# Turning the last two products of a decode block around: weights as the moving operand, four column groups

## The chip, the cores and the metric

One core of one Trainium2 chip. The metric is device time in microseconds (us); lower is better. Times are medians of several executions, and all of them are fast unless a line says otherwise. A ratio of two kernels is the mean time of one kernel's fast runs over the mean of the other's in the same rounds on the same chip, so it is not quite the ratio of the medians that are quoted. All intervals are 95%.

## The reference, cut to what matters

A gated mix of a cached attention block and a mixer MLP, for two rows (batch 2, one position), D = 1024, 32 heads of 128, 16384 cached keys a head, F = 3584, everything in bf16:

```python
g = sigmoid((x * gate_w).sum(-1, keepdims=True))
a = attention(x @ wq, k_cache, v_cache).reshape(B, Sq, H * Dh) @ wo      # wo: 4096 x 1024
x1 = x + shift_mix(gelu(layernorm(x) @ w1)) @ w2
b = x1 + gelu(layernorm(x1) @ w3) @ w4                                  # w4: 3584 x 1024
return g * a + (1 - g) * b
```

The two caches are 537 MB of the 573 MB that are read. The two products at the end, with `w4` and `wo`, give two rows of 1024 outputs. Of a matmul's two operands, the kernel's `lhsT` is called *stationary* here and its `rhs` *moving*; the page lists the load of the stationary one as PEld and the matmul itself as PE, 5589 of each before the change. The sums stand in tiles of the pools in PSUM.

## The kernel before

Everything that is loaded in bulk goes through a ring of three buffers of 64 KB a partition (`big`). A load *lands* when the last of its records of completion comes in the trace; the trace lists each load as *packets*, which the 16 DMA engines move; here a packet is one contiguous piece.

```python
    const = ctx.enter_context(tc.tile_pool(name="const", bufs=1))
    big = ctx.enter_context(tc.tile_pool(name="big", bufs=NBIG))
    tpool = ctx.enter_context(tc.tile_pool(name="tpool", bufs=2))
    # ... cut: other pools
    def load_k(i):
        t = big_tile("Kn")
        nc.sync.dma_start(
            out=t[:].rearrange("p (j d) -> p j d", d=Dh), in_=cache_rows(A_k_cache, i)
        )
    # ... cut
    W4_SPLIT = [7] * 4
    WO_SPLIT = [4] * 6 + [2, 2, 1, 1, 1, 1]     # rows of 256 KB per DMA
```

The tail: `st_down` multiplies by `w4`, the result is added to the residual `x1` and weighted by `1 - g` into `pre`; `wo_stage` multiplies by `wo` and takes `pre` in through the identity. The weights are the stationary operand, and the two batch rows are the moving one: eight matmuls of two columns a weight row.

```python
    def wo_stage():
        # ... cut: Q, the attention rows, transposed and permuted
        wo = wt.pop("wo").rearrange("k r (p c) -> k r p c", c=KC)
        for r in range(32):
            if r == 24:
                nc.tensor.matmul(wo_acc[:]..., lhsT=ident_f[:], rhs=pre[:]..., start=False, stop=False)
            for c in range(KC):
                nc.tensor.matmul(
                    wo_acc[:, c, :], lhsT=wo[:, r, :, c], rhs=Q[:, :, r],
                    start=(r == 0 and c == 0), stop=(r == 31 and c == KC - 1),
                )
    # ...
    xn2T = const.tile([P, KC, B], BF16)
    h2T = const.tile([P, FC, B], BF16)
    pre = const.tile([P, KC, B], FP32)

    def st_down():
        # ... cut: the same eight matmuls a row, with w4 and h2T, into ps
        nc.vector.tensor_tensor(out=pre[:], in0=x1[:], in1=ps[:], op=ALU.add)
        nc.vector.tensor_tensor(out=pre[:], in0=pre[:], in1=over_r(omg_bc[:]), op=ALU.mult)
    # ... at the very end
    out_pm = const.tile([P, B, KC], BF16)
    nc.vector.tensor_copy(out=out_pm[:].rearrange("p b r -> p r b"), in_=wo_acc[:])
    nc.sync.dma_start(out=out.rearrange("b s (p r) -> p (b s) r", p=P), in_=out_pm[:])
```

## Time and profile before

| | before |
|---|---|
| time, median | 1338.44 us |
| span of the profiled run | 1336.7 us |
| read from HBM | 573 MB at 428 GB/s |
| last row of `wo` lands | 1331.84 us |
| last matmul ends | 1333.26 us |
| output DMA issued | 1333.54 us |

The page gives busy time as shares of the span, and then the span in 40 slices; a digit is the busy share of a slice in tenths.

```profile
PE 845.2 (63%) x5589; PEld 403.1 (30%) x5589; DVE 709.2 (53%) x863; ACT 45.6 (3%) x100; POOL 14.2 (1%) x45
...
DMA  9999999999999999999999999999999999999997
...
q1 hardware_dynamic: 12928, 572.54, 99.1%
q8 instruction: 44, 0.72, 0.2%
```

The DMA line is what matters: the 16 DMA engines are busy from end to end, and no compute engine is. The last two lines are queues (packets, MB, share of 16 engines' span): all loads are on one queue of 12928 packets, and the other one, which the page calls `instruction`, carries 44 packets.

The timeline of the tail (start, duration, engine, line, operation, count, and in brackets the idle time before and what ended it):

```profile
1321.91 2.09 PE L406 MATMUL wo_acc<-Q,wo 128*128 128x2 bf16 x32 [0.34 <-DMA wo<-in_A_wo_dram]
1324.36 2.09 PE L406 MATMUL wo_acc<-Q,wo 128*128 128x2 bf16 x32 [0.35 <-DMA wo<-in_A_wo_dram]
1326.80 2.10 PE L406 MATMUL wo_acc<-Q,wo 128*128 128x2 bf16 x32 [0.35 <-DMA wo<-in_A_wo_dram]
1328.76 0.59 PE L398 MATMUL wo_acc<-pre,ident_f 128*128 128x16 f32 x2
1329.19 4.05 PE L406 MATMUL wo_acc<-Q,wo 128*128 128x2 bf16 x64
1333.28 0.23 DVE L557 CAST out_pm<-wo_acc 128x16 bf16<-128x16 f32 x1 [17.16 <-PE wo_acc L406]
1333.54 0.40 SPq L559 DMA_DIRECT2D out_dram<-out_pm  x1
```

And the chain that ended last, from 1303.63 us (start, duration, what):

```profile
1303.63 23.12 DMA wo<-in_A_wo_dram
1326.75 0.05 issue
1326.80 2.10 PE wo_acc L406 x32
1328.90 0.45 PE wo_acc L398 x2
1329.35 3.91 PE wo_acc L406 x64
1333.26 0.02 issue
1333.28 0.23 DVE out_pm L557
```

Up to 1326.75 us the chain is a load. After it PE has no bracket, so it waits for nothing: it has fallen behind the last, small pieces and works them off until 1333.26 us, 1.4 us after the last row has landed. That 1.4 us, the copy and the output are all that is not load time.

### The profile page before, as it was taken

The page shows a single profiled execution, that of the slowest core. Times are in us where ns is not written, and L with a number is a line of the kernel's source. Part 1 is how long each engine was busy: PE and PEld are TensorE (multiplying, and loading weights), DVE is VectorE, ACT ScalarE, POOL GpSimd, SP SyncE. Part 2 cuts the span into 40 slices and gives each one's busy share as a digit, 9 for nine tenths or more (in the row PEclk, how much of TensorE's full clock was granted, in tenths as well). Part 3 has the DMA queues.
Part 4 walks back from the last instruction along what each step waited for, and adds up shares of the span by engine and source line. Part 5 has one row for each costly group of instructions (what it writes and reads, how often), then busy time and mean ns, then how long its engine had stood idle before and what let it go on. Part 6 is the DMA issues. An engine that isn't in the chain of part 4 may idle for free.

```text
span 1336.7 us, 12996 instructions
## 1 busy us (share of the span) xinstructions
PE 845.2 (63%) x5589; PEld 403.1 (30%) x5589; DVE 709.2 (53%) x863; ACT 45.6 (3%) x100; POOL 14.2 (1%) x45
## 2 busy tenths in 40 slices
PE   2577665677657765555766555567656556765568
PEld 2233222433225322222322222233222223322238
DVE  0666565366651665545666545556655455656520
ACT  0000000000000000000000000000000000000000
POOL 0000000000000000000000000000000000000000
PEclk9988777688776877778887777888777788877775
DMA  9999999999999999999999999999999999999997
GB/s 409 436 436 434 422 440 434 429 440 434 422 435 437 440 436 422 430 440 428 438 438 433 430 432 430 440 438 426 434 430 438 438 432 430 434 428 436 434 421 294
DMA packets 12986, 573.37 MB, mean 429 GB/s; under 512 B 2048, under 2 KB 2048, under 8 KB 2816
## 3 DMA queue, kind: packets, MB, share of 16 engines
q1 hardware_dynamic: 12928, 572.54, 99.1%
q8 instruction: 44, 0.72, 0.2%
q14 instruction: 14, 0.11, 0.0%
HBM read 572.53 MB, written 0.00 MB: 428 GB/s over the span
## 4 chain that ended last, share of the span: by engine, by line
PE 29%; DVE 24%; DMA 17%; another core or an unknown queue 14%; issue 13%; ACT 3%; SPq 0%; ACTq 0%; POOL 0%
DVE T L297 20%; PE S L305 15%; DMA Kn<-in_A_k_cache_dram 13%; PE O L349 7%; PE misc L212 2%; PE misc L359 2%; DMA w<-in_B_w_dram 2%; DMA wo<-in_A_wo_dram 2%; PE misc L458 2%; ACT Pr L333 1%; DVE PT L337 1%; ACT Os L357 1%; DVE mx L326 1%; DVE mdiag L319 1%
## 5 line engine op out<-in xcount | busy, mean ns | idle before, releaser
L305 PE MATMUL S<-T,z 128*128 128x512 bf16 x2048 | 596.1, 424 | 325.0 <-DVE T L297 309.9
L297 DVE STREAM_TRANSPOSE T<-Kn 128x1024 f32<-128x1024 f32 x512 | 612.1, 1230 | 264.6 <-DMA Kn<-in_A_k_cache_dram 215.3
L305 PEld LDWEIGHTS <-z 128*128 128x128 bf16 x2048 | 218.7, 107 | 696.9 <-issue 535.0
L349 PE MATMUL O<-Vn,PT 128*32 128x512 bf16 x2048 | 121.4, 390 | 5.0 <-DMA Vn<-in_A_v_cache_dram 5.0
L376 DVE SCALAR_TENSOR_TENSOR OT<-misc,g_bc,rinv 128x2 bf16<-128x2 f32 x32 | 7.0, 220 | 159.2 <-PE misc L359 159.2
L349 PEld LDWEIGHTS <-PT 128*32 128x32 bf16 x2048 | 73.8, 140 | 51.3 <-issue 22.1
L212 PE MATMUL misc<-rs,ones_f 128*128 128x2 f32 x64 | 17.9, 349 | 79.1 <-DVE rs L369 79.1
L357 ACT COPY Os<-O 128x512 f32<-128x512 f32 x32 | 18.8, 586 | 1067.1 <-PE O L349 1067.1
L359 PE MATMUL misc<-osel,Os 128*128 128x2 f32 x256 | 34.5, 257 | 22.2 <-ACT Os L357 22.2
L359 PEld LDWEIGHTS misc<-osel,Os 128*128 128x128 f32 x256 | 31.8, 195 | 37.1 <-ACT Os L357 37.1
L316 DVE TENSOR_REDUCE m<-S 128x1 f32<-128x512 f32 x32 | 22.1, 692 | 36.9 <-PE S L305 36.9
L212 PEld LDWEIGHTS misc<-rs,ones_f 128*128 128x128 f32 x64 | 16.1, 312 | 84.0 <-issue 81.2
L337 DVE STREAM_TRANSPOSE PT<-Pr 128x512 bf16<-128x512 bf16 x32 | 22.8, 711 | 28.7 <-ACT Pr L333 28.7
L212 PE MATMUL misc<-mdiag,ones_f 128*128 128x128 f32 x64 | 15.6, 326 | 16.9 <-DVE mdiag L319 16.9
L333 ACT ACTIVATE Pr<-S,nb 128x512 bf16<-128x512 f32 x32 | 22.0, 687 | 125.2 <-DVE nb L328 122.2
L458 PEld LDWEIGHTS <-wt 128*128 128x128 bf16 x352 | 22.3, 165 | 9.8 <-DMA wt<-in_B_w_dram 8.5
L326 DVE TENSOR_REDUCE mx<-misc 64x1 f32<-64x64 f32 x64 | 14.2, 222 | 18.9 <-PE misc L212 18.5
L250 PE MATMUL misc<-xT,wt 128*128 128x2 bf16 x256 | 7.1, 165 | 25.8 <-DVE xT L245 23.2
L275 POOL TENSOR_TENSOR z<-qsel,own 128x32 bf16<-128x32 bf16 x32 | 10.6, 330 | 1205.4 <-PE S L305 1174.2
L458 PE MATMUL misc<-xn2T,wt 128*128 128x2 bf16 x224 | 14.4, 202 | 8.3 <-DMA wt<-in_B_w_dram 8.3
L373 DVE RECIPROCAL rinv<-misc 128x2 f32<-128x2 f32 x32 | 5.5, 171 | 22.6 <-PE misc L212 22.6
L406 PE MATMUL wo_acc<-Q,wo 128*128 128x2 bf16 x256 | 16.3, 199 | 1.1 <-DMA wo<-in_A_wo_dram 1.1
(76 smaller groups left out, 119.5 us busy)
## 6 DMA issues: line engine op xcount, KB each, us to landing
Vn<-in_A_v_cache_dram SPq DMA_DIRECT2D x2, 4096.0 KB, 47.3
wt<-in_B_w_dram SPq DMA_DIRECT2D x1, 7168.0 KB, 50.3
w<-in_B_w_dram SPq DMA_DIRECT2D x4, 1792.0 KB, 29.1
wo<-in_A_wo_dram SPq DMA_DIRECT2D x6, 1024.0 KB, 30.2
wt<-in_B_w_dram SPq DMA_DIRECT2D x2, 2048.0 KB, 39.6
wo<-in_A_wo_dram SPq DMA_DIRECT2D x2, 512.0 KB, 18.6
wo<-in_A_wo_dram SPq DMA_DIRECT2D x4, 256.0 KB, 12.7
Kn<-in_A_k_cache_dram SPq DMA_DIRECT2D x32, 51.9
```

The lines of the kernel that those rows point to most:

```text
L212: nc.tensor.matmul(ps[:], lhsT=ones_f[:], rhs=src, start=True, stop=True)
L297: nc.vector.transpose(out=T[:].rearrange("p w j s -> p j w s"), in_=Kw[:, m * CW : (m + 1) * CW].rearrange("p (j w e) -> p j w e", w=2, e=32),
L305: nc.tensor.matmul(S[:], lhsT=z[:, v, NM - 1 - m : NM - 1 - m + P], rhs=Tb[:, v // 2, :, v % 2], start=(m == 0 and v == 0), stop=(m == NM ...
L316: nc.vector.reduce_max(out=m[:], in_=S[:], axis=AX.X)
L326: nc.vector.reduce_max(out=mx[pa, :], in_=mall[pa, pa], axis=AX.X)
L333: nc.scalar.activation(out=Pr[:], in_=S[:], func=ACTF.Exp, bias=nb[:], scale=scale, accum_out=rs[:])
L337: nc.vector.transpose(out=PT[:], in_=Pr[:])
L349: nc.tensor.matmul(O[32 * g : 32 * g + 32, :], lhsT=PT[:, m : CJ * 32 : 16], rhs=V[:, j0 : j0 + 4, :], start=(m == 0), stop=(m == NM - 1),)
L357: nc.scalar.copy(out=Os[:].rearrange("p x d -> p (x d)"), in_=O[:])
L359: nc.tensor.matmul(oc[:], lhsT=Os[:, x, :], rhs=osel[:, x, :], start=(x == 0), stop=(x == 3))
L406: nc.tensor.matmul(wo_acc[:, c, :], lhsT=wo[:, r, :, c], rhs=Q[:, :, r], start=(r == 0 and c == 0), stop=(r == 31 and c == KC - 1),)
L458: nc.tensor.matmul(ps[:, c, :], lhsT=w[:, r, :].rearrange("k (p c) -> k p c", c=C)[:, :, c], rhs=actT[:, r, :], start=(r == 0), stop=(r == ...
```

## The change

Its intent: let the weights move instead. A weight row then needs four matmuls of 256 moving columns with a stationary operand of only two columns, and the four write from partitions 0, 32, 64 and 96 on; they are called four column groups here. Both products, and the residual, add up in one PSUM tile. The residual goes in early, through small fp32 matmuls right after `x1` is known, and `1 - g` is multiplied into the gelu. The output leaves as eight rows of 512 bytes, on two queues.

```diff
     OT = const.tile([P, B, H], BF16)
-    wo_acc = acc.tile([P, KC, B], FP32, name="wo_acc")
+    NQ = 4
+    QW = D // NQ
+    out_acc = acc.tile([P, QW], FP32, name="out_acc")
@@
+    def add_row_product(actT, w_row, last=False):
+        for g in range(NQ):
+            nc.tensor.matmul(
+                out_acc[group(g), :],            # partitions 32g and 32g + 1
+                lhsT=actT,
+                rhs=w_row[:, g * QW : (g + 1) * QW],
+                start=False, stop=last, skip_group_check=True,
+            )
+
+    def start_out(x1):
+        # ... cut: four matmuls that clear out_acc
+        res = const.tile([P, KC, B], FP32, name="cen")
+        nc.vector.tensor_tensor(out=res[:], in0=x1, in1=over_r(omg_bc[:]), op=ALU.mult)
+        # ... cut: 32 fp32 matmuls, res against the identity, into out_acc
@@
-        # ... cut: the loop over r and c of wo_stage
+        for r in range(32):
+            add_row_product(Q[:, :, r], wo[:, r, :], last=(r == 31))
@@
-    pre = const.tile([P, KC, B], FP32)
@@ st_down
+        for r in range(FC):
+            add_row_product(h2T[:, r, :], w4[:, r, :])
@@
-    out_pm = const.tile([P, B, KC], BF16)
-    # ... cut: copy and one output DMA
+    rows = t_tile([P, QW], BF16, "rows")
+    nc.vector.tensor_copy(out=rows[:], in_=out_acc[:])
+    for b, queue in enumerate((nc.sync, nc.scalar)):
+        queue.dma_start(
+            out=out[b].rearrange("s (g n) -> (s g) n", g=NQ), in_=rows[b : 96 + b + 1 : 32, :]
+        )
```

More of the change, by code (lines that the diff above doesn't have):

```diff
@@ L383, in pv_stage, with group @@
         )
+    def group(g):
+        return slice(32 * g, 32 * g + B)
+    def add_row_product(actT, w_row, last=False):
[4 more added lines that the diff above has]
+                rhs=w_row[:, g * QW : (g + 1) * QW],
+                start=False,
+                stop=last,
+                skip_group_check=True,
+            )
+    def start_out(x1):
+        for g in range(NQ):
+            nc.tensor.matmul(
+                out_acc[32 * g : 32 * g + 32, :],
+                lhsT=perm[:, 0:32],
+                rhs=shT[:, 0, 0:1].to_broadcast([P, QW]),
+                start=True,
+                stop=False,
+                skip_group_check=True,
+            )
+        res = const.tile([P, KC, B], FP32, name="cen")
+        nc.vector.tensor_tensor(out=res[:], in0=x1, in1=over_r(omg_bc[:]), op=ALU.mult)
+        for c in range(KC):
+            for g in range(NQ):
+                nc.tensor.matmul(
+                    out_acc[group(g), c:QW:KC],
+                    lhsT=res[:, c, :],
+                    rhs=ident_f[:, 32 * g : 32 * g + 32],
+                    start=False,
+                    stop=False,
+                    skip_group_check=True,
+                )
     def wo_stage():
@@ L394, in wo_stage @@
         nc.vector.tensor_copy(out=Q[:], in_=q_ps[:])
-        wo = wt.pop("wo").rearrange("k r (p c) -> k r p c", c=KC)
+        wo = wt.pop("wo")
         for r in range(32):
-            if r == 24:
-                nc.tensor.matmul(
-                    wo_acc[:].rearrange("p c b -> p (c b)"),
-                    lhsT=ident_f[:],
-                    rhs=pre[:].rearrange("p c b -> p (c b)"),
-                    start=False,
-                    stop=False,
-                )
-            for c in range(KC):
-                nc.tensor.matmul(
-                    wo_acc[:, c, :],
-                    lhsT=wo[:, r, :, c],
-                    rhs=Q[:, :, r],
-                    start=(r == 0 and c == 0),
-                    stop=(r == 31 and c == KC - 1),
-                )
+            add_row_product(Q[:, :, r], wo[:, r, :], last=(r == 31))
     def layernorm(src, dst):
@@ L436, in layernorm, with gelu @@
         nc.vector.tensor_tensor(out=dst, in0=cen[:], in1=over_r(rstd[:]), op=ALU.mult)
-    def gelu(pre_f32, dst_bf, C):
+    def gelu(pre_f32, dst_bf, C, weight=None):
         sq = t_tile([P, C, B], FP32, "gelu")
@@ L448, in gelu @@
         )
+        if weight is not None:
+            nc.vector.tensor_tensor(
+                out=sq[:], in0=sq[:], in1=weight.unsqueeze(1).to_broadcast([P, C, B]), op=ALU.mult
+            )
         nc.vector.tensor_tensor(out=dst_bf, in0=sq[:], in1=pre_f32, op=ALU.mult)
@@ L486, in st_mix @@
         layernorm(x1[:], xn2T[:])
+        start_out(x1[:])
     def st_up():
@@ L490, in st_up @@
         nc.vector.tensor_copy(out=h2[:], in_=linear("w3", xn2T)[:])
-        gelu(h2[:], h2T[:], FC)
+        gelu(h2[:], h2T[:], FC, omg_bc[:])
     def st_down():
-        w4 = wt.pop("w4").rearrange("k r (p c) -> k r p c", c=KC)
-        ps = misc_psum([P, KC, B])
+        w4 = wt.pop("w4")
         for r in range(FC):
-            for c in range(KC):
-                nc.tensor.matmul(
-                    ps[:, c, :],
-                    lhsT=w4[:, r, :, c],
-                    rhs=h2T[:, r, :],
-                    start=(r == 0 and c == 0),
-                    stop=(r == FC - 1 and c == KC - 1),
-                )
-        nc.vector.tensor_tensor(out=pre[:], in0=x1[:], in1=ps[:], op=ALU.add)
-        nc.vector.tensor_tensor(out=pre[:], in0=pre[:], in1=over_r(omg_bc[:]), op=ALU.mult)
+            add_row_product(h2T[:, r, :], w4[:, r, :])
     extra = {
@@ L554 @@
     assert not xfers
-    out_pm = const.tile([P, B, KC], BF16)
-    nc.vector.tensor_copy(out=out_pm[:].rearrange("p b r -> p r b"), in_=wo_acc[:])
-    with nc.allow_non_contiguous_dma(reason="4 KB"):
-        nc.sync.dma_start(out=out.rearrange("b s (p r) -> p (b s) r", p=P), in_=out_pm[:])
+    rows = t_tile([P, QW], BF16, "rows")
[3 more added lines that the diff above has]
+            out=out[b].rearrange("s (g n) -> (s g) n", g=NQ), in_=rows[b : 96 + b + 1 : 32, :]
+        )
 _INS = ['A_x', 'A_k_cache', 'A_v_cache', 'A_wq', 'A_wo', 'B_x', 'B_w1', 'B_w2', 'B_w3', 'B_w4', 'gate_w']
```

## The prediction

> **What bounds the kernel now.** Loads. The page shows the 16 DMA engines at 9 tenths or more in 39 of 40 slices, 573 MB at 429 GB/s; PE is busy 63%, DVE 53%. The DMA issues show that a K load is issued 51.9 us and a V load 37.4 us before it lands, while 8.4 MB take about 19 us: work is always queued ahead. Only the stretch after the last landing belongs to compute.
>
> **The tail, from the timeline and the DMA issues in narrow windows.** The wo pieces land at about 1324.3, 1326.75, 1328.0, 1329.2, 1329.85, 1330.6, 1331.2 and, the last row, 1331.9. PE works without a wait from 1326.80 to 1333.25: rows 24 to 31 are 64 matmuls in 4.05 us (0.51 us a row of eight), with the two-pass residual matmul, 0.45 us, ahead of them. PE ends 1.35 us behind the last landing. Then DVE copies 128x16 (0.23 us), and the output DMA, issued at 1333.54, lands 2.4 us later. Granted clock is 0.5 there.
>
> **What the change does.**
> - w4 and wo: 480 matmuls of 2 moving columns become 240 of 256, four to a row in four column groups. The O matmuls run this pattern: at a cold clock 32 of 512 columns took 3.64 us, 0.455 us per four. [...] Estimate for 256 columns: 0.23 to 0.27 us a row, against 0.51 before and a row landing every 0.6 us. PE catches up with the loads; after the last landing four matmuls are left, about 0.4 us. It ends near 1332.3 instead of 1333.25. Gain 0.9 us.
> - Residual: two DVE operations on `pre` (0.17 us each) and the late 0.45 us matmul go. About 70 small PE instructions come near 260 us, an estimated 4 to 6 us. DVE there waits 6.85 us for the next K load, so they fit: no cost. The extra multiply in the second gelu, about 0.2 us: no cost.
> - The last copy is 128x256: 0.43 us, an estimate from the 128x512 PSUM reduction (692 ns). Cost 0.2 us.
> - Output: 256 elements of 16 bytes in one DMA become eight of 512 bytes on two queues: 2.4 us becomes perhaps 2.0 to 2.2. Gain 0.2 to 0.4 us.
> - Instruction loads: the DMA records show 16 KB instruction packets (about 0.9 us of one engine each), one every 8 us in the tail. With half the PE instructions there, two of four vanish; the last landing may come 0 to 0.6 us earlier. Gain 0.2 us, uncertain.
>
> Nearly all of the 15 us or so of PE time saved was hidden under loads.
>
> **Prediction.** 1337.2 us, 8 in 10 between 1336.1 and 1338.4. Faster by over 2%: 0.01; within 2%: 0.98; slower by over 2%: 0.01.
>
> **What would show it.** Right: PE waits for a wo DMA before nearly every late piece; rows at 0.22 to 0.3 us; last PE instruction within 0.6 us of the last landing; loads unchanged; the chain of waits ends with a wo DMA, then PE under 1 us. Wrong: rows near 0.9 us would mean column groups one after the other; a gap in the DMA slices near 260 to 300 us would mean that the new start of the sum delayed a buffer.
>
> **What could make it wrong.** A last landing moved by over 1 us through instruction loads or engine imbalance; serial column groups (estimate: about 20 us later); a larger fixed cost of an output DMA on the ScalarE queue.

The gains and costs come to 1.1 to 1.3 us (0.9 - 0.2 + 0.2 to 0.4 + 0.2), and 1338.4 less 1.2 is the 1337.2 us of the forecast. The "cold clock" of the O matmuls was a granted clock of 0.50 (`before`, 1295.1 to 1299.0 us). Of the estimates, the 4 to 6 us of the residual fit 63 ns for each of 70 matmuls (the tail's 64 took 4.05 us), and the 20 us of serial groups fit 60 rows at 0.9 us where one lands every 0.6 us (18 us). That the output DMA would take 2.0 to 2.2 us, and that two of four late instruction packets would vanish, were guesses.

## The result, and the profile after

1341.29 us (median of 4; 1341.07 to 1341.67) against 1338.45 us (1338.41 to 1338.84): ratio 1.0021, interval 1.0003 to 1.0038. Within 2%, as forecast, but 2.8 us slower instead of 1.2 us faster, and outside the stated range.

The page, same lines (the second queue of output is new):

```profile
PE 830.6 (62%) x5415; PEld 380.9 (28%) x5415; DVE 709.3 (53%) x863; ACT 45.6 (3%) x100; POOL 14.5 (1%) x45
...
DMA  9999999999999999999999999999999999999997
...
q1 hardware_dynamic: 12664, 572.54, 99.1%
q8 instruction: 42, 0.69, 0.2%
...
q10 hardware_dynamic: 8, 0.00, 0.0%
```

The tail's timeline, with the middle left out:

```profile
1328.03 1.02 PE L392 MATMUL out_acc<-wo,Q 128*2 128x256 bf16 x16 [1.42 <-DMA wo<-in_A_wo_dram]
...
1330.49 1.02 PE L392 MATMUL out_acc<-wo,Q 128*2 128x256 bf16 x16 [1.44 <-DMA wo<-in_A_wo_dram]
...
1334.96 0.38 PE L392 MATMUL out_acc<-wo,Q 128*2 128x256 bf16 x4 [0.27 <-DMA wo<-in_A_wo_dram]
...
1335.60 0.39 PE L392 MATMUL out_acc<-wo,Q 128*2 128x256 bf16 x4 [0.25 <-DMA wo<-in_A_wo_dram]
...
1336.04 0.42 DVE L575 CAST rows<-out_acc 128x256 bf16<-128x256 f32 x1 [31.21 <-PE out_acc L392]
1336.49 0.65 SPq L577 DMA_DIRECT2D out_dram<-rows  x1
1336.49 1.35 ACTq L577 DMA_DIRECT2D out_dram<-rows  x1
```

The end of the chain:

```profile
1325.56 10.00 DMA wo<-in_A_wo_dram
1335.56 0.04 issue
1335.60 0.41 PE out_acc L392 x4
1336.01 0.02 issue
1336.04 0.42 DVE rows L575
```

Compute did what was intended. Sixteen matmuls (four rows) now take 1.02 us instead of 2.09 us for the 32 matmuls of before, PE waits for every late piece, and it ends 0.45 us after the last landing instead of 1.4. But the last landing itself moved from 1331.84 to 1335.56 us. The reason is not in the tail, as the SyncE queue's timeline shows. It lists when loads are issued; a load is issued when its buffer is freed, which follows the landings before it (in `before`, SyncE waits 584.6 us at the V loads for DVE's work on a K tile, and 333.2 us for K to land). Before:

```profile
32.93 0.33 SPq L106 DMA_DIRECT2D Vn<-in_A_v_cache_dram  x1
...
95.42 0.33 SPq L95 DMA_DIRECT2D Kn<-in_A_k_cache_dram  x1
...
697.14 0.33 SPq L95 DMA_DIRECT2D Kn<-in_A_k_cache_dram  x1
...
1204.12 0.33 SPq L95 DMA_DIRECT2D Kn<-in_A_k_cache_dram  x1
...
1276.02 1.75 SPq L130 DMA_DIRECT2D w<-in_B_w_dram  x4
```

After:

```profile
33.03 0.33 SPq L106 DMA_DIRECT2D Vn<-in_A_v_cache_dram  x1
...
95.88 0.33 SPq L95 DMA_DIRECT2D Kn<-in_A_k_cache_dram  x1
...
699.34 0.33 SPq L95 DMA_DIRECT2D Kn<-in_A_k_cache_dram  x1
...
1206.53 0.33 SPq L95 DMA_DIRECT2D Kn<-in_A_k_cache_dram  x1
...
1279.34 1.75 SPq L130 DMA_DIRECT2D w<-in_B_w_dram  x4
```

Line by line, the loads are issued later by 0.10, 0.46, 2.2, 2.4 and 3.3 us: they fall behind over the whole span. Issue times are a rough measure (one V load is issued 0.45 us *earlier*, at 160.88 instead of 161.33 us). The times of landing grow evenly: against the padded kernel of experiment 2, whose loads run as before the change, a load's last landing is later by 0.2 us at 63 us, 0.3 at 198, 0.85 at 403, 1.3 at 614 and 3.2 at 1275. All of this precedes the first instruction with `w4`. The records of the single DMA packets in the trace say the same. Their durations were almost constant before and are not any more:

| packets, over the whole span after 20 us | before | after |
|---|---|---|
| 64 KB load packets, mean | 2421.4 ns | 2424.7 ns |
| share of them at 2418 ns or less | 98% | 17% |
| 16 KB instruction packets, mean | 927 ns (44) | 1063 ns (42) |

### The profile page after: what moved, and what is told of

It reads as the page before. It is cut to its first block, busy times and chain, and to the rows that moved or that the text cites. A ratio compares the mean times of both kernels' runs of the same rounds, so it can differ in the third digit from the quotient of the medians.

```text
span 1339.3 us, 12650 instructions
## 1 busy us (share of the span) xinstructions
PE 830.6 (62%) x5415; PEld 380.9 (28%) x5415; DVE 709.3 (53%) x863; ACT 45.6 (3%) x100; POOL 14.5 (1%) x45
## 4 chain that ended last, share of the span: by engine, by line
PE 27%; DVE 24%; DMA 19%; another core or an unknown queue 14%; issue 13%; ACT 3%; SPq 0%; ACTq 0%; POOL 0%
DVE T L299 20%; PE S L307 14%; DMA Kn<-in_A_k_cache_dram 13%; PE O L351 7%; DMA Vn<-in_A_v_cache_dram 3%; DMA wo<-in_A_wo_dram 3%; PE misc L212 2%; PE misc L361 2%; PE misc L486 2%; ACT Pr L335 1%; DVE PT L339 1%; ACT Os L359 1%; DVE mx L328 1%; DVE mdiag L321 1%
```

## The experiments

The first two theories. **Theory Q:** the change put an output DMA on a second queue (ScalarE's), and the DMA engines, serving one more queue, take a little longer over every packet. **Rival I:** it is something in the changed program itself: PE's instructions, their loads, or where things lie in memory.

### 1. Which queue: a_sync, b_out_act, b_gate_act, b_out_pool

`a_sync`, on the changed kernel:

```diff
-    for b, queue in enumerate((nc.sync, nc.scalar)):
+    for b, queue in enumerate((nc.sync, nc.sync)):
```

> The changed kernel with both output DMAs on the SyncE queue; nothing else differs from it. Theory Q (the second DMA queue makes every load packet a little slower through the whole span): the 64 KB packets return to 2418 ns in nearly all cases, the last wo landing returns from 1335.6 to about 1331.9 us, and the time is 1337.0 to 1338.0 us, ahead of the kernel before by 0.5 to 1.4 us. Rival I (the changed PE program, its instruction loads and its placement in memory slow the loads): still 1340.8 to 1341.8 us.

Measured: 1341.64 us against 1338.69 us (ratio 1.0022, interval 1.0008 to 1.0036). Packets as after the change: mean 2424.8 ns, 18% at 2418 ns or less. One queue is just as slow.

`b_out_act`, on the kernel before:

```diff
-        nc.sync.dma_start(out=out.rearrange("b s (p r) -> p (b s) r", p=P), in_=out_pm[:])
+        nc.scalar.dma_start(out=out.rearrange("b s (p r) -> p (b s) r", p=P), in_=out_pm[:])
```

> The kernel before, its one output DMA moved from the SyncE queue to the ScalarE queue; nothing else. Theory Q: 64 KB packets spread from 2418 to 2418-2427 ns, the last wo landing 3 to 4 us later, time 1341.3 to 1342.5 us. Rival I: no change, 1338.2 to 1338.8 us.

Measured: 1338.73 us against 1338.69 us (ratio 1.0000), packets at 2418 ns (98%).

`b_gate_act`, on the kernel before:

```diff
-            nc.sync.dma_start(out=gw_pm[:], in_=gate_w.rearrange("(p r) -> p r", p=P))
+            nc.scalar.dma_start(out=gw_pm[:], in_=gate_w.rearrange("(p r) -> p r", p=P))
```

> The kernel before, with its 2 KB load of gate_w on the ScalarE queue at the start; output on SyncE as before. Tells whether it is the existence of a second queue or the DMA at the end. Theory Q (existence is enough): 1341 to 1342.5 us, packets slower in the whole span. If only a late DMA matters: 1338.2 to 1338.8 us. Rival I: 1338.2 to 1338.8 us.

Measured: 1338.41 us against 1338.69 us (ratio 0.9998).

`b_out_pool`: as `b_out_act`, with `nc.gpsimd`.

> The kernel before, its output DMA issued by GpSimd instead of SyncE. Theory Q in its plain form (any second queue costs the loads about 3.5 us): last wo landing 3 to 4 us later and 1341 to 1343 us, with perhaps 1 us more for the output itself. If only a second queue of the same kind as the loads' costs: last landing at 1331.9 us and 1338.5 to 1340 us.

Measured: 1338.92 us against 1338.69 us (ratio 1.0002). The 1 us more for the output was a guess, and it does not show.

Theory Q falls with all four. One small DMA on a second queue costs the loads nothing here, whether it comes at the start or at the end.

### 2. Where the load buffers lie: a_pad96, b_pad32, b_pad64, b_base0

What else differs between the two kernels from the first loads on? No instruction does that matters there; but addresses do. The change removed two small constants, `pre` (64 bytes a partition) and `out_pm` (32 bytes; its successor lives in another pool). The constants lie in front of the load ring, so the three load buffers moved 96 bytes: from byte 20736 of each partition to 20640. (These are the addresses that the compiler gave.) 20736 is 81 times 256; 20640 is 32 past a multiple of 64.

**Theory S:** loads into a buffer that starts off some multiple (64 or more) are slower. Rival I keeps everything else of the changed program.

`a_pad96`, on the changed kernel:

```diff
     h2T = const.tile([P, FC, B], BF16)
+    pad = const.tile([P, 48], BF16, name="pad")
```

> The changed kernel as it is (output on two queues), with an unused tile of 96 bytes a partition among the constants. The change had removed 96 bytes of constants (pre 64, out_pm 32) and so moved the three load buffers from byte 20736 of a partition (a multiple of 64) to 20640 (32 past one); the pad puts them back. Theory S (loads into a buffer that starts 32 bytes past a multiple of 64 are a little slower): 64 KB packets at 2418 ns again, last wo landing near 1331.9 us, time 1336.8 to 1338.0 us, ahead of the kernel before by 0.5 to 1.5 us. Rival I (the changed PE program, its instruction loads, or where the program lies in memory): still 1341 to 1342 us.

Measured: 1337.45 us (1337.28 to 1337.48) against 1338.38 us (1338.07 to 1338.86); ratio 0.9992, interval 0.9980 to 1.0005. Packets: mean 2421.3 ns, 98% at 2418 ns. The pad, an unused tile, takes back the whole loss. Its SyncE queue and its end of the chain:

```profile
1204.13 0.33 SPq L95 DMA_DIRECT2D Kn<-in_A_k_cache_dram  x1
...
1276.11 1.75 SPq L130 DMA_DIRECT2D w<-in_B_w_dram  x4
```

```profile
1321.86 9.96 DMA wo<-in_A_wo_dram
1331.82 0.04 issue
1331.86 0.41 PE out_acc L392 x4
1332.27 0.02 issue
1332.29 0.42 DVE rows L576
```

The issue times are those of before to 0.1 us, the last landing is back at 1331.82 us, and what follows it is as short as after the change.

`b_pad32` and `b_pad64`, on the kernel before: the same line with 16 and with 32 elements, so that the buffers start at 20768 and 20800.

> The kernel before with an unused tile of 32 bytes a partition: load buffers at 20768, 32 past a multiple of 64; no engine's program differs otherwise. Theory S: 64 KB packets spread over 2418 to 2427 ns, mean about 2424.7; last landing 3 to 4 us later; 1341.3 to 1342.8 us. Rival I: 1338.2 to 1338.9 us.

Measured: 1343.14 us against 1338.38 us (ratio 1.0035, interval 1.0022 to 1.0048), packets 2425.8 ns. So the unchanged kernel loses 4.8 us by an unused tile of 32 bytes.

> The kernel before with an unused tile of 64 bytes: load buffers at 20800, a multiple of 64 but not of 128 or 256. Theory S with a grain of 64 bytes: as before, 1338.2 to 1338.9 us, packets at 2418 ns. With a grain of 128 or more: 1341 to 1343 us. Rival I: as before.

Measured: 1342.40 us (ratio 1.0030, interval 1.0018 to 1.0043), packets 2424.9 ns. A multiple of 64 is not enough.

`b_base0`, on the kernel before: `Q1`, `Q` and `out_pm` taken from the constants into the pool of `T`, and a pad of 32 bytes; buffers at 20480, a multiple of 512.

> The kernel before with three small late tiles moved to another pool and a pad of 32 bytes, so that the load buffers start at 20480, a multiple of 512 (20736 was a multiple of 256 alone). Theory S with a grain of 64: as before, 1338.2 to 1338.9 us. A coarser grain that the kernel before already missed: faster by 1 us or more, packets under 2418 ns. Rival I: as before.

Measured: 1338.59 us against 1338.38 us (ratio 1.0001), packets 2421.4 ns. A multiple of 512 gains nothing over one of 256.

### 3. The loads or the rest, and the grain: b_loads64, b_rest64, b_base128, a_pad96_sync

A pad among the constants moves the load buffers and every later tile alike. The next two move one without the other, both starting from `b_base0`. A pool `gap` of one tile, opened between `big` and `tpool`, makes up the difference. **Rival T:** the small tiles count.

```diff
# b_loads64                                              # loads at 20544, the rest from 217344 on, as before
-    pad = const.tile([P, 16], BF16, name="pad")
+    pad = const.tile([P, 48], BF16, name="pad")
+    gap_tile = gap.tile([P, 96], BF16, name="gap")
# b_rest64                                               # loads at 20480, the rest from 217152 on
+    gap_tile = gap.tile([P, 32], BF16, name="gap")
```

> The kernel before with the three load buffers alone moved: they start at 20544, a multiple of 64 but not of 128; the tiles behind them (T, Pr, PT, statistics) are back at 221440, as before. Theory S (where the loads are written is what counts): slow as with the 64-byte pad, 1341.5 to 1343 us, 64 KB packets mean about 2425 ns. Rival T (the small tiles that the engines work on count, and load packets only suffer from it): 1338.0 to 1339.0 us.

Measured: 1342.30 us against 1338.33 us (ratio 1.0029, interval 1.0017 to 1.0042), packets 2424.9 ns.

> The counterpart: load buffers at 20480, a multiple of 512; the tiles behind them moved by 64 bytes to 221248. Theory S: 1338.0 to 1339.0 us, packets at 2418 ns. Rival T: 1341.5 to 1343 us.

Measured: 1338.45 us (ratio 1.0001), packets 2421.2 ns. So it is the load buffers alone. Moving a buffer moves what is written there and what the compute engines read there; the trace tells these apart. In `b_pad64` no compute engine has an instruction between 1293.8 and 1298.7 us (PE waits for the last piece of V), while packets of `w4` go on arriving. Of the 88 packets of 14 KB that lie between 1294 and 1298.2 us one took 535 ns or less; before, in the same wait (1290.5 to 1295.2 us), 90 of 92 did. The packets are slow with nobody reading. The SyncE queue of the two runs shows the delay in mid-span; `b_loads64`:

```profile
698.90 0.33 SPq L96 DMA_DIRECT2D Kn<-in_A_k_cache_dram  x1
...
1207.08 0.33 SPq L96 DMA_DIRECT2D Kn<-in_A_k_cache_dram  x1
```

and `b_rest64`, which differs from it in the sizes of the two pads alone:

```profile
697.12 0.33 SPq L96 DMA_DIRECT2D Kn<-in_A_k_cache_dram  x1
...
1204.16 0.33 SPq L96 DMA_DIRECT2D Kn<-in_A_k_cache_dram  x1
```

The same K loads are issued 1.8 us later at 697 us and 2.9 us later at 1204 us.

`b_base128`: as `b_base0`, with a pad of 160 bytes; buffers at 20608, a multiple of 128 but not of 256.

> The kernel before with load buffers at 20608, a multiple of 128 but not of 256. If the grain is 128 bytes: 1338.0 to 1339.0 us and packets at 2418 ns; if it is 256: 1341.5 to 1343 us.

Measured: 1342.06 us (ratio 1.0028, interval 1.0016 to 1.0041), packets 2424.6 ns. Of the starts tried, 20480 and 20736 are fast, and 20544, 20608, 20640, 20768 and 20800 are slow, which fits a grain of 256 bytes. How far past a multiple the start lies does not set the cost: at 32, 64, 128 and 160 bytes past, the mean 64 KB packet took 2425.8, 2424.9, 2424.6 and 2424.7 ns.

`a_pad96_sync`: `a_pad96` with both output DMAs on SyncE.

> The changed kernel with the 96-byte pad and both output DMAs on SyncE. With the loads undisturbed this sizes the output alone: the second DMA waits for the issue of the first (0.65 us in the trace), so 0.2 to 0.7 us slower than the padded kernel with two queues: 1337.6 to 1338.2 us.

Measured: 1337.85 us against 1338.33 us (ratio 0.9996, interval 0.9982 to 1.0009). On its own chip it is 0.5 us faster than before; `a_pad96`, on another chip, was 0.9 us faster. The second queue is thus worth about 0.4 us (an estimate across two chips), and it is harmless.

### 4. Once a packet, or by the byte: p16k, p16k_off64, s4, s4_off64

Does a start off a multiple of 256 cost once for each packet, whatever its size, or by the byte? Kernels with smaller packets and the same bytes tell the two apart. The first pair of kernels put four pieces of 16 KB on each partition, with two DMAs a tile, one a head:

```diff
+        for a in range(G):
+            nc.sync.dma_start(
+                out=t[64 * a : 64 * a + 64, :].rearrange("p (c x) -> p c x", c=4),
+                in_=cache[b, hg * G + a].rearrange("(c p j) d -> p c (j d)", c=4, p=64),
+            )
```

> The kernel before with its K and V loads in four pieces of 16 KB a partition instead of one of 64 KB (other cache rows on each partition, the same for K and V, so the result is the same; two DMAs a tile, one a head); load buffers at 20736, a multiple of 256. This is the aligned reference of the next run; its own time is only roughly expected: four times the packets at 611 ns each instead of 2418 would be 1% more, so 1338 to 1355 us.

> The same with load buffers at 20800 (the 64-byte pad). With 64 KB packets this pad cost 4.0 us. If a start off a multiple of 256 costs once a packet [...]: four times the packets, 9 to 17 us more than p16k. If it costs by the byte written: about 4 us more than p16k (3 to 5).

Measured: 2682.6 us for the first (four runs; one run took 2633.9), 2692.5 us for the second. Both expectations of the first run were missed: the loads fell to half their rate, and 16 KB packets took 1259 ns on average instead of 611. Why was not followed up. With that, the pair decides nothing.

The second pair keeps the rows of a partition together and only issues each tile in quarters (`s4`), with the 64-byte pad on top (`s4_off64`):

```diff
-        nc.sync.dma_start(
-            out=t[:].rearrange("p (j d) -> p j d", d=Dh), in_=cache_rows(A_k_cache, i)
-        )
+        tv = t[:].rearrange("p (j d) -> p j d", d=Dh)
+        src = cache_rows(A_k_cache, i)
+        for j0 in range(0, NJ, NJ // 4):
+            nc.sync.dma_start(out=tv[:, j0 : j0 + NJ // 4, :], in_=src[:, j0 : j0 + NJ // 4, :])
```

(and the same for V, by its list of splits.)

> The kernel before with each K and V load issued as four DMAs, one after the other, of a quarter of the rows each: the packets become 16 KB, and each DMA still reads all 128 partitions' rows at the pitch of before (unlike the run with two heads, whose loads fell to half rate). Load buffers at 20736, a multiple of 256. Aligned reference of the next run. Packets near 611 ns, as those of 16 KB in wq: 1345 to 1365 us by four times 611 against 2418.

> The same with load buffers at 20800 (the 64-byte pad). Cost per packet: the packets of 16 KB take 3 to 5 ns more each, as those of 64 KB did (3.5 ns), and the time is 8 to 17 us above s4. Cost per byte: about 1 ns a packet, and 3 to 5 us above s4.

Measured: 1346.06 us and 1356.22 us, against 1338.68 us for the kernel before on that chip. The pad costs 10.2 us instead of 4.0, with the same bytes: the cost goes with the packets. The recorded times of the load packets, summed up and divided by 16 engines, rise by 8.4 us instead of 2.55, a factor of 3.3, and there are 35,328 of them instead of 10,880, a factor of 3.2. The pages of the two runs, first `s4`:

```profile
q1 hardware_dynamic: 40432, 572.55, 99.7%
...
GB/s 397 428 431 431 430 430 431 431 430 430 431 435 426 429 432 432 429 429 433 431 429 431 431 430 429 433 430 430 431 431 429 432 429 432 430 431 429 430 430 305
```

then `s4_off64`:

```profile
q1 hardware_dynamic: 40432, 572.55, 99.6%
...
GB/s 397 428 426 429 428 427 428 427 427 428 427 437 420 426 429 428 425 430 427 427 428 427 428 429 426 427 429 426 428 429 427 426 430 427 427 428 427 428 425 291
```

The same packets and bytes, 2 to 5 GB/s less in most slices. The packet records agree, within one kernel too. With the 64-byte pad, the mean packet took more by

| packet size | 8 KB | 16 KB | 32 KB | 64 KB | 16 KB in s4 |
|---|---|---|---|---|---|
| more, in ns | 5.1 | 3.7 | 4.4 | 3.6 | 3.7 |

that is, about the same from 8 to 64 KB (14 KB: 3.6; at 4 and 2 KB it is 1.8 and 4.9, but a few long packets make much of these means). So the cost is once a packet. What it is inside the packet is not shown. Nor is it one fixed amount in every packet: with the 64-byte pad the most frequent duration of 64 KB packets is 2420 ns, 2 ns above 2418, and the second most frequent is 2427 ns, 9 ns above.

And the lengthening is not there from the start. Of the 64 KB packets that start between 20 and 40 us, 63% take 2418 ns or less in `b_pad64`, no fewer than in the kernels with fast starts (52 to 78%); between 40 and 80 us it is 74% against 87 to 97%, and from 240 us on 5 to 6% against 99%. A fixed addition to each packet would cost the first packets as much as the last, so that is not all of it; the mechanism stays open.

## Why the prediction was wrong

The forecast sum had five terms. `a_pad96` runs the same change with the load buffers where they were, and tells them apart.

- **"Loads unchanged", the unwritten term of the sum, is the step that failed.** The prediction took the last landing to stay where it was (it had 1331.9 us), or to come up to 0.6 us earlier. It came at 1335.56 us. The runs show in its place that removing 96 bytes of constants moved the load buffers off a multiple of 256 bytes, which makes the mean 64 KB load packet about 3.3 ns longer. There are 10,880 load packets of 2 KB or more, 680 for each of 16 engines, so that is an estimated 2.2 us of each engine's time; the recorded packet times, summed up and divided by 16, rise by 2.2 us too. The last landing moved by 3.7.

  The rest lies between the DMA engines. Each load leaves 16 records of completion, as many as there are DMA engines, and we take them as one each. For the third last piece of `wo` the earliest of the 16 moved from 1321.32 to 1323.57 us, by 2.25, which is what the packets give, and the latest from 1330.54 to 1334.27, by 3.73: the spread grew from 9.2 to 10.7 us. Before the change, too, seven of the records of that piece lie within 0.6 us and the other nine 7 to 9.2 us behind them, and over the span the latest falls back in steps of 0.4 to 1.1 us, most of them between two landings in which an instruction packet of 16 KB ran. The mean of these packets rose from 927 to 1063 ns (in the runs with 64 KB packets it was 927 to 936 ns with fast starts and 1056 to 1068 ns with slow ones). So the missing 1.5 us is the late engines'; that it comes of the instruction packets is argued, not shown, as the kept trace does not say which engine a packet ran on.

  The forecast named the risk "a last landing moved by over 1 us" through instruction loads or engine imbalance. Neither was the trigger, since `a_pad96` has the same instruction packets (42) and no delay, but part of the delay does show as imbalance.
- **PE at the tail, gain 0.9 us: right.** A row of four matmuls takes 0.24 to 0.26 us (28 matmuls in 1.66 us, 16 in 1.02) at granted clock 0.50 (`after`, 1328.0 to 1329.1 us); estimated were 0.23 to 0.27. PE ends at 1332.27 us in `a_pad96`; estimated was 1332.3. The four column groups do run at once. In `before`, at granted clock 0.50 (307.1 to 311.0 us), full-array matmuls of 512 columns start 0.43 us apart, one at a time; O matmuls of 512 columns, at 0.50 too (1295.1 to 1299.0 us), start in fours within 0.07 us of each other, and the fours 0.43 us apart. The 32 of them took 3.64 us, 0.455 us per four; four in turn would be an estimated 1.7 us (4 times 0.43). Rows near the 0.9 us of serial groups were not seen.
- **The last copy, cost 0.2 us: right.** 0.42 us, estimated 0.43.
- **The output, gain 0.2 to 0.4 us: right.** From issue to the end of the span it took 3.16 us before (1333.54 to 1336.7) and 2.76 us in `a_pad96` (1332.74 to 1335.5), 0.4 us less.
- **The residual, no cost: right; its size was not.** The fp32 products took 1.03 us of PE instead of the estimated 4 to 6 us, and the clears ran at 2.2 us, before the first loads had landed. Nothing waited for either.
- **Instruction loads, gain 0.2 us: not seen.** There are 42 of these packets instead of 44, and the last landing of `a_pad96` is within 0.1 us of before.

The terms that concern compute add up to what the padded kernel shows: 1337.45 us, 0.9 us less than the kernel before in its rounds, against 1.2 us forecast. The interval of the ratio (0.9980 to 1.0005) does not exclude equality, though the two sets of runs do not overlap. If the padded kernel is better than the kernel before, it is by less than 0.1%.

## What to carry to other kernels

In a kernel bound by loads, list which tiles the change adds to or removes from the pools that lie in front of the load buffers, and check where those buffers start: a start off a multiple of 256 bytes cost 3.7 to 4.8 us of 1338 here (3.8 in the changed kernel, against its padded form), and 10 us with packets of 16 KB, more than the change itself could gain. When loads get slower though no load was touched, compare the times of the same load along the whole span: a delay that grew all along, as here, is a rate, and its cause need not be where the new instructions run. A pad of unused bytes takes a minute to try and separates addresses from instructions. Look, too, at the spread of a load's completion records: in the kernel before, those of the third last piece of `wo` average 4.7 us before the latest, so engines that ended together could bring the last landing forward by an estimated 4 to 5 us, more than this change aimed at. No run tried it.
